# Retention and a gated feed-forward block on one core: another order of the last output products, and of two weight loads at the start

## The chip, the core and the metric

The program runs on one core of a Trainium2 chip. The core has five engines with queues of their own that run at the same time and wait for each other by semaphores. TensorE (PE in the profile; PEld is its loading of weights) multiplies matrices and writes only to PSUM, an accumulating memory of eight banks. VectorE (DVE) does elementwise work, ScalarE (ACT) copies and functions such as softplus and erf, GpSimd (POOL) elementwise work too. SyncE (SP) issues DMA transfers, ScalarE's queue can issue some as well. "SPq" and "ACTq" stand for these queues. Data lie in SBUF, 128 partitions wide; inputs and outputs in DRAM.

The metric is the device time of one execution in microseconds.

## The reference

```python
# attention: 8 batches, 8 heads, 576 tokens, head dim 64
scores = scale * np.matmul(q, k.transpose(0, 1, 3, 2))
gamma = 1.0 - 2.0 ** (-5.0 - np.arange(H))
Dmat = np.where(rel >= 0, gamma ** rel, 0.0)       # rel = position of q - position of k
x = matmul(scores * Dmat, v)                       # -> (4608 tokens, 512)
# feed-forward
h = x @ w_in                                       # 512 -> 2048
sp = np.maximum(h, 0.0) + np.log1p(np.exp(-np.abs(h)))
g = h * erf(sp)
out = g @ w_out                                    # 2048 -> 512
```

q, k and v are float32. w_in and w_out come as 64-bit floats, and the kernel gets them as raw words: it makes float32 of them itself, which the code calls rounding.

## The kernel before, in words

**Attention.** The 4608 tokens are 36 pieces of 128 (each ninth piece is two rests of 64 tokens). A piece goes through three stages: `transposes` (q and k of the piece are turned on TensorE, line 332, or from piece 8 on in part on VectorE, line 326), `scores` (line 347, then VectorE's masking into `sT`, line 99 through the helper `tt`), and `outputs` (lines 365, 376, 388, with a state that is carried from piece to piece). `outputs` writes the piece's columns of `x`, four pieces to a chunk of 512 tokens, nine chunks. The list `stages` fixes the order: transposes of piece i+1, outputs of i, scores of i+1 (outputs first for pieces 5 and 7). `transposes(i)` asks for q of piece i+2, `outputs(i)` for k and v of piece i+3. Each is two DMAs on SyncE's queue (line 147), of 128 KB each; q has two buffers in turn, k and v four. From piece 8 on q, and from piece 12 on k, come in other pieces (line 131).

**Feed-forward.** w_in's 2048 columns are worked in four groups `g` of 512; for each group all nine chunks are passed. `First` is the stage x @ w_in with what follows it up to g, `Second` the product with w_out, added to an output tile `o` that goes through DRAM (`od`) from group to group. Most of these products are done as seven products of half-size blocks, with sums of blocks before and after (names such as A11, S1, B21, T2). `First.plain`, used for the first two chunks of group 0, is the ordinary product instead: sixteen steps, four for each 128 rows of w_in (`dc` 0 to 3). It can so begin with the first part of w_in while the others still come.

**Weights.** `parts()` lists the pieces of weights: for each group four parts of w_in (128 rows, two DMAs of 256 KB, line 237) and four of w_out (one DMA of 512 KB). `load_weights` asks for the next part, into one of four buffers `wraw`. `round_weights(5)` makes one part into float32 with ScalarE (lines 254, 255) and VectorE (lines 259, 263, 267, 272), and for w_in of group 0 two more operations on VectorE (lines 274, 275), else on GpSimd.

**Order at the start.** Everything up to the end of the first chunk's plain product is in an order written out by hand, a string read character by character: "a" is the next stage of attention, "p" a step of the plain product, "w" `load_weights`, a digit so many steps of `round_weights`, "k" two idle matmuls that keep TensorE busy, "l" a load of k and v, "c" the second half of the constants, "s" a store of x. Nothing reorders instructions after that; each engine and each queue takes its own in program order.

**The end.** Line 806 runs the last second stage: chunk 8 of group 3. `first` gives the products B11 and B21, `rest` then T2, T3, T1, T4 and B22. Each product is four calls of 128x256 matmuls on TensorE (line 604; eight records in the profile), into a PSUM bank that holds two blocks of 128 tokens (`tp` 0 and 1), each 256 columns wide. B11, T2, T1 and B22 accumulate in bank `a`, B21 in bank `e`, T3 and T4 in bank `g`. After each product one VectorE addition of 128x512 (`take` or `add`, line 99) adds the bank to `o`. `store` writes results to the output in DRAM (line 688 for this chunk): columns 0 to 255 of half 0 on ScalarE's queue after T3, half 1 on SyncE's after T4, the rest of half 0 on both queues after B22.

Of the kernel before, what the change touches and what calls it, by code (L numbers as in the profile page):

```python
# [11 lines left out]
FP32 = mybir.dt.float32  # L12
# [3 lines left out]
ALU = mybir.AluOpType  # L16
PSUM = bass.MemoryType.PSUM

P = 128
B, H, S, D = 8, 8, 576, 64  # L20
D_MODEL, D_FF = 512, 2048
NP = H // 2
# [32 lines left out]
def kernel(  # L55
# [10 lines left out]
    nc = tc.nc  # L66
# [3 lines left out]
    TH = TCH // 2  # L70
    n_ch = n_tok // TCH
    n_dc = D_MODEL // P
    OH = D_MODEL // 2
    FH = D_FF // 2
    GP = 2
# [14 lines left out]
    ps_at = ctx.enter_context(tc.tile_pool(name="ps_at", bufs=4, space=PSUM))  # L90
# [7 lines left out]
    def tt(out, in0, in1, op):  # L98
        nc.vector.tensor_tensor(out=out, in0=in0, in1=in1, op=op)  # L99

    def flat(ap):
        return ap.rearrange("p h d -> p (h d)")
# [47 lines left out]
    def load(i, names="qkv"):  # L150
        if i < len(pieces):
            t = loaded.setdefault(i, {})
            for name in names:
                src = {"q": q, "k": k, "v": v}[name]
                if name == "q" and i < SQUARES:
                    t["q"] = load_rows(i, "q", q, 2)
                elif name == "q":
                    t["qs"] = load_squares(i, "q", q)
                    if i >= SQUARES_K:
                        t["ks"] = load_squares(i, "k", k)  # L160
                elif name == "v" or i < SQUARES_K or len(pieces[i]) == 1:
                    t[name] = load_rows(i, name, src, 4)
# [19 lines left out]
    B11, T3, B21, B22, T1, T2, T4 = range(7)  # L182
    weights = {}
# [48 lines left out]
    def load_weights():  # L232
        part = next(coming, None)
        if part is not None:
            t = wraw.tile([P, 2 * WP], UINT32, tag="wraw", name="wraw")
            for rows, src in part[0]:
                nc.sync.dma_start(out=t[rows].rearrange("p (h f) -> p h f", h=2), in_=src)
            words.append((t, *part[1:]))
# [49 lines left out]
    def round_weights(n=1):  # L288
        for _ in range(n):
            next(round_step, None)  # L290
# [151 lines left out]
    def before_chunk(c):  # L442

        return stages.index((outputs, c * PC)) if c < n_ch else len(stages)

    def after_chunk(c):

        return stages.index((outputs, (c + 1) * PC - 1)) + 1

    def attend(upto):  # L450
        while done[0] < min(upto, len(stages)):
            of, i = stages[done[0]]
            of(i)
            done[0] += 1
# [5 lines left out]
    def load_x(g, c):  # L460
        x[g, c] = x_tile()
        nc.sync.dma_start(out=x[g, c][:, :n_dc], in_=xd[c])

    def store_x(c):
        nc.sync.dma_start(out=xd[c], in_=x[0, c][:, :n_dc])
# [3 lines left out]
    def operands_x(g, c):  # L469
        summed.add((g, c))  # L470
        t = x[g, c]
        b11, b12, b21, b22 = (t[:, 2 * d : 2 * d + 2, h * TH : (h + 1) * TH] for d in range(2) for h in range(2))
        t1, t2, t4 = (t[:, n_dc + j, :].rearrange("p (d i) -> p d i", d=2) for j in range(3))
        if g == 0 or c < PLAIN:
            tt(t1, b12, b11, ALU.subtract)
            tt(t2, b22, t1, ALU.subtract)
            tt(b12, b22, b12, ALU.subtract)
        else:
            tt(t2, b12, b11, ALU.add)
            tt(t1, b22, t2, ALU.subtract)  # L480
        if g == 0:
            store_x(c)
        tt(t4, b21, t2, ALU.subtract)
        x[g, c] = {A11: b11, A12: b21, S4: b22, A22: t4, S1: t1, S2: t2, S3: b12}
# [102 lines left out]
    class Second:  # L587
# [58 lines left out]
        def last(self):  # L646
# [6 lines left out]
            self.store(1)  # L653
            yield

        def rest(self):


            e = ps_e.tile([P, 2, OH], FP32, tag="g", name="g2")
            self.product(T2, self.a, False)  # L660
            self.take(1, 0, self.a)
            yield
            self.product(T3, e, True)
            self.add(1, 1, e)
            self.store(0, slice(0, OH), nc.scalar)
            yield
            self.product(T1, self.a, False)
            self.take(1, 1, self.a)
            yield
            self.product(T4, e, False)  # L670
            self.add(1, 0, e)
            self.store(1)
            yield
            self.product(B22, self.a, False)
            self.take(0, 1, self.a)
            for tp, queue in enumerate((nc.sync, nc.scalar)):
                self.store(0, slice(OH, D_MODEL), queue, (tp,))
            yield
# [29 lines left out]
    def keep_busy(n):  # L708
        for _ in range(n):
            nc.tensor.matmul(idle[:, :P], lhsT=ones, rhs=ones, start=True, stop=True)  # L710
# [4 lines left out]
    def run(steps, rounds=(), stages=1):  # L715

        for step, _ in enumerate(steps):
            attend(min(done[0] + stages, most[0]))
            round_weights(rounds[step] if step < len(rounds) else 0)
# [4 lines left out]

    for what in "alkakakawkakakawaa3awwa2aaa5ppappawwppa5ppaw5appwcppa5ppaaapp5s":
        if what == "a":
            attend(done[0] + 1)
        elif what == "p":  # L730
            next(products)
        elif what == "s":
            store_x(0)
        elif what == "l":
            load(2, "kv")
        elif what == "c":
            nc.sync.dma_start(out=cst[:, CONST_FIRST:], in_=consts[:, CONST_FIRST:])
        elif what == "w":
            load_weights()
        elif what == "k":  # L740
            keep_busy(2)
        else:
            round_weights(int(what))
# [18 lines left out]
    for b, nxt in zip(blocks[2:], blocks[3:] + [None]):  # L762
        n = order.index((b.g, b.c))
        if isinstance(b, First):
            most_g[0] = order[n - 1][0] + 1
            run(b.middle(), (1, 1) if n != 2 else ())
            firsts[n - 1].sums()
            run(seconds[n - 1].first(), (1, 1) if n > 2 else ())
            run(b.last(), (1,) if 2 < n < n_ch else ())
            if n in (2, 3):  # L770
                load_weights()
            most[0] = before_chunk(n + 3)
        elif n + 2 < n_s:
            f = firsts[n + 1]
            for step, _ in enumerate(b.middle()):
                attend(min(done[0] + 1, most[0]))
                if step == 0:
                    f.erf()
                elif step == 1 and (n + 2 >= n_ch or done[0] == len(stages)):
                    operands_x(*order[n + 2])  # L780
                elif step == 2 and n_ch - 4 < n < n_ch:
                    round_weights()
            if order[n + 2] not in summed:
                attend(after_chunk(n + 2))
                operands_x(*order[n + 2])
            run(nxt.first(), (1,) if n > 1 else ())
            f.multiply()
            seconds[n + 1].begin()
            if n_ch <= n + 3 < n_s:
                load_x(*order[n + 3])  # L790
            run(b.last(), (0, 1) if n > 1 else ())
        elif n + 1 < n_s:
            firsts[n + 1].erf()
            seconds[n + 1].begin()
            rest = b.rest()
            for _ in range(3):
                next(rest)
            firsts[n + 1].multiply()
            run(rest)
            firsts[n + 1].sums((0,))  # L800
            first = nxt.first()
            next(first)
            firsts[n + 1].sums((1,))
            run(first)
        else:
            run(b.rest())


# [28 lines left out]
```

## Time and profile before

| | us |
|---|---|
| median of eight runs (1026.51 to 1031.78) | 1027.68 |
| profiled execution, own time | 1031.78 |
| profiled execution, span | 1030.0 |
| TensorE busy | 1019.2 |
| VectorE busy | 668.9 |
| ScalarE busy | 390.3 |
| GpSimd busy | 124.1 |
| one product of a second stage, chain on TensorE | 1.73 |
| addition of 128x512 on VectorE, in the groups `o<-a,o` | 0.69 |

The page has busy times by engine, and a strip of 40 equal slices of the span (25.75 us each):

```profile
PE   9989999999999999999999999999999999999998
PEld 8778888888888888888888888888888888888887
DVE  3858877877876666666566666666667655555555
ACT  2254133232244544343343344444443333333332
POOL 2133121221311110000001001100100000000000
PEclk9999999999999999999999999999999999999999
DMA  9998979979984444444445344444333334444433
```

A digit is the busy share of the slice in tenths. PEclk is the clock that TensorE was granted, in tenths. DMA is the share of the sixteen DMA engines. Attention's stages lie between the products in the first slices up to about 270 us; after that only feed-forward is left. A TensorE that is shown as busy can still be slower than it could be, since ends of matmuls are modelled.

### The profile page before, as it was taken

To read this page: it belongs to the slowest core of one execution; us is meant where nothing else is said; L and a number is where in the kernel's file an instruction comes from. 1 tells how busy PE (TensorE), PEld (TensorE's weight loads), DVE (VectorE), ACT (ScalarE), POOL (GpSimd) and SP (SyncE) were. 2 spreads that over 40 slices of the span, in tenths; PEclk is the share of its full clock that TensorE was granted. 3 is DMA by queue.
4 is the path that set the end of the run, shared out by engine and by line. 5 is a ranking of instruction groups with operands and counts; after the bars stand their busy time and mean duration, and the time that the engine had idled before them with its cause. 6 is when DMAs were issued, how large, how long until landed. Compare 5 with 4: busy or idle time off the path is not lost.

```text
span 1030.0 us, 15950 instructions
## 1 busy us (share of the span) xinstructions
PE 1019.2 (99%) x6348; PEld 876.7 (85%) x6348; DVE 668.9 (65%) x1055; ACT 390.3 (38%) x481; POOL 124.1 (12%) x122
## 2 busy tenths in 40 slices
PE   9989999999999999999999999999999999999998
PEld 8778888888888888888888888888888888888887
DVE  3858877877876666666566666666667655555555
ACT  2254133232244544343343344444443333333332
POOL 2133121221311110000001001100100000000000
PEclk9999999999999999999999999999999999999999
DMA  9998979979984444444445344444333334444433
GB/s 194 182 238 184 231 165 241 236 170 247 221 192 150 163 143 143 143 163 163 162 144 172 137 143 147 159 165 143 143 123 123 123 127 131 130 131 133 125 95 110
DMA packets 146986, 165.76 MB, mean 161 GB/s; under 512 B 97376, under 2 KB 121568, under 8 KB 138848
## 3 DMA queue, kind: packets, MB, share of 16 engines
q1 hardware_dynamic: 144848, 163.70, 55.9%
q10 hardware_dynamic: 2064, 1.05, 0.4%
q8 instruction: 50, 0.82, 0.3%
q14 instruction: 24, 0.20, 0.1%
HBM read 117.52 MB, written 47.19 MB: 160 GB/s over the span
## 4 chain that ended last, share of the span: by engine, by line
PE 87%; DMA 6%; SPq 3%; DVE 2%; issue 1%; ACT 0%; POOL 0%; DVEq 0%; ACTq 0%; POOLq 0%
PE a L604 23%; PE a L496 22%; PE g L604 11%; PE g L496 11%; PE e L604 6%; PE e L496 5%; PE s L347 2%; PE o L365 2%; SPq L147 2%; DMA raw_k<-in_k_dram 1%; DMA raw_ks<-in_k_dram 1%; DMA raw_qs<-in_q_dram 1%; DMA wraw<-in_moe_w_in_dram 1%; PE o L388 1%; PE p L550 1%; PE o L376 1%
## 5 line engine op out<-in xcount | busy, mean ns | idle before, releaser
L496 PE MATMUL a<-x,wa 128*128 128x256 f32 x1088 | 258.3, 380 | 0.0
L496 PEld LDWEIGHTS a<-x,wa 128*128 128x128 f32 x1088 | 205.7, 190 | 28.5
L604 PE MATMUL a<-wb,s 128*128 128x256 f32 x864 | 205.7, 381 | 0.0
L604 PEld LDWEIGHTS a<-wb,s 128*128 128x128 f32 x864 | 162.9, 190 | 23.6 <-ACT o L618 0.7
L99 DVE TENSOR_TENSOR t<-g,t 128x512 f32<-128x512 f32 x68 | 47.0, 691 | 150.5 <-ACT t L526 113.0
L496 PE MATMUL g<-x,wa 128*128 128x256 f32 x544 | 129.2, 380 | 0.0
L496 PEld LDWEIGHTS g<-x,wa 128*128 128x128 f32 x544 | 102.8, 190 | 14.4
L99 DVE TENSOR_TENSOR o<-a,o 128x512 f32<-128x512 f32 x108 | 74.3, 688 | 49.2 <-PE a L604 49.2
L521 ACT COPY t<-a 128x512 f32<-128x512 f32 x34 | 19.9, 586 | 188.3 <-PE a L496 188.3
L99 DVE TENSOR_TENSOR t<-t,s 128x1024 f32<-128x1024 f32 x72 | 88.9, 1276 | 0.0
L565 ACT ACTIVATE s<-t 128x1024 f32<-128x1024 f32 x72 | 72.1, 1049 | 27.8 <-DVE t L99 27.8
L274 POOL TENSOR_TENSOR wraw<-wraw 128x512 f32<-128x512 f32 x28 | 29.4, 1050 | 438.5 <-DVE wraw L272 179.1
L99 DVE TENSOR_TENSOR x<-x 128x512 f32<-128x512 f32 x115 | 75.8, 693 | 1.2
L532 ACT COPY t<-a 128x512 f32<-128x512 f32 x34 | 19.9, 586 | 144.4 <-PE a L496 144.4
L569 ACT ACTIVATE s<-s 128x1024 f32<-128x1024 f32 x72 | 72.1, 1048 | 0.4
L604 PE MATMUL g<-wb,s 128*128 128x256 f32 x288 | 68.6, 381 | 0.0
L604 PE MATMUL e<-wb,t 128*128 128x256 f32 x288 | 68.5, 380 | 0.0
L604 PE MATMUL a<-wb,t 128*128 128x256 f32 x288 | 68.5, 380 | 0.0
L604 PE MATMUL g<-wb,t 128*128 128x256 f32 x288 | 68.2, 380 | 0.0
L99 DVE TENSOR_TENSOR sT<-s,cst 128x512 f32<-128x512 f32 x72 | 46.2, 682 | 30.7 <-PE s L347 28.5
L99 DVE TENSOR_TENSOR o<-g,o 128x512 f32<-128x512 f32 x72 | 49.4, 686 | 24.6 <-ACT o L618 19.8
L496 PE MATMUL e<-x,wa 128*128 128x256 f32 x272 | 64.8, 381 | 0.0
(76 smaller groups left out, 1229.1 us busy)
## 6 DMA issues: line engine op xcount, KB each, us to landing
od<-o SPq DMA_DIRECT2D x54, 512.0 KB, 3.3
x<-xd SPq DMA_DIRECT2D x27, 1024.0 KB, 4.8
o<-od SPq DMA_DIRECT2D x27, 1024.0 KB, 4.9
raw_qs<-in_q_dram SPq DMA_DIRECT2D x96, 112.0 KB, 4.5
raw_ks<-in_k_dram SPq DMA_DIRECT2D x84, 112.0 KB, 4.2
xd<-x SPq DMA_DIRECT2D x9, 1024.0 KB, 4.9
raw_v<-in_v_dram SPq DMA_DIRECT2D x64, 128.0 KB, 4.6
wraw<-in_moe_w_in_dram SPq DMA_DIRECT2D x32, 256.0 KB, 5.9
```

The costliest lines, as they stand in the source:

```text
L99: nc.vector.tensor_tensor(out=out, in0=in0, in1=in1, op=op)
L147: queue.dma_start(out=t[r0 : r0 + n, e::2, :], in_=heads.rearrange("h p d -> p h d"))
L274: engine.tensor_tensor(out=r_f, in0=high_f, in1=r_f, op=ALU.mult)
L347: nc.tensor.matmul(ps[e][:, p, :], lhsT=t["kT"][heads[e], p, :], rhs=t["qT"][heads[e], p, :], start=True, stop=True)
L365: nc.tensor.matmul(o[p % 2][heads[(e + p) % 2], p // 2, :], lhsT=t["v"][:, 2 * p + e, :], rhs=t["sT"][:, e, p, :], start=(p < 2), stop=(no ...
L376: nc.tensor.matmul(o[p % 2][heads[(e + p) % 2], p // 2, r0 : r0 + m], lhsT=state[heads[e], p, :], rhs=t["qT"][heads[e], p, r0 : r0 + m], s ...
L496: nc.tensor.matmul(acc[:, j * TH : (j + 1) * TH], lhsT=weights["wa", self.g][:, a, d, j * P : (j + 1) * P], rhs=x[self.g, self.c][a][:, d, :],
L521: nc.scalar.copy(out=self.t1[:, 1], in_=self.a)
L532: nc.scalar.copy(out=self.t2[:, 0], in_=self.a)
L565: nc.scalar.activation(self.s[:, j], t, AF.Softplus)
L569: nc.scalar.activation(self.s[:, j], self.s[:, j], AF.Erf)
L604: nc.tensor.matmul(acc[:, tp, :], lhsT=left[:, j * TH + tp * P : j * TH + (tp + 1) * P], rhs=weights["wb", self.g][:, b, j, :], start=(sta ...
```

## The change

Two things are changed. At the start, three characters of the string move. "w" for the third part of w_in comes directly after that for the second, ahead of the loads of q, k and v of piece 5; the fourth keeps its place. The rounding of the third part ("5") comes before the scores of piece 5 instead of after them, and that of the fourth after those scores, before the outputs of piece 5, instead of after the outputs. TensorE's own order at the start stays as it was.

At the end, `final` replaces `first` and `rest` for the last second stage. The products keep their order, but the two blocks of 128 tokens have banks of their own: two banks for B11, T2, T1 and B22 and two for B21, T3 and T4, all from the pool `ps_at` that attention has used before. For each product block 0 is done whole, then block 1; each has its own addition of 128x256. The stores are by block as well: block 0 on SyncE's queue, block 1 on ScalarE's, after B21 (half 0, columns 0 to 255), T4 (half 1) and B22 (half 0, the other columns).

```diff
+        def final(self):
+            a = [ps_at.tile([P, NP, P], FP32, tag="at", name=f"f{tp}") for tp in range(2)]
+            e = [ps_at.tile([P, NP, P], FP32, tag="at", name=f"h{tp}") for tp in range(2)]
+            steps = [(B11, a, 0, 0), (B21, e, 0, 0), (T2, a, 1, 0), (T3, e, 1, 1)]
+            steps += [(T1, a, 1, 1), (T4, e, 1, 0), (B22, a, 0, 1)]
+            for n, (b, banks, half, oh) in enumerate(steps):
+                left = self.of.left[b]
+                for tp in range(2):
+                    acc = flat(banks[tp])[:, :OH]
+                    for j in range(GP):
+                        nc.tensor.matmul(
+                            acc,
+                            lhsT=left[:, j * TH + tp * P : j * TH + (tp + 1) * P],
+                            rhs=weights["wb", self.g][:, b, j, :],
+                            start=(b in (B11, B21, T3) and j == 0),
+                            stop=(j == GP - 1),
+                            skip_group_check=True,
+                        )
+                    dst = self.o[:, half, tp, oh * OH : (oh + 1) * OH]
+                    tt(dst, acc, dst, ALU.add)
+                    if b in (B21, T4, B22):
+                        cols = slice(0, D_MODEL) if half == 1 else slice(oh * OH, (oh + 1) * OH)
+                        self.store(half, cols, (nc.sync, nc.scalar)[tp], (tp,))
+                yield n
...
-    for what in "alkakakawkakakawaa3awwa2aaa5ppappawwppa5ppaw5appwcppa5ppaaapp5s":
+    for what in "alkakakawkakakawwaa3awa2aaa5ppappa5wwppa5ppawappwcppa5ppaaapp5s":
...
-            first = nxt.first()
-            next(first)
+            steps = nxt.final()
+            next(steps)
             firsts[n + 1].sums((1,))
-            run(first)
+            next(steps)
         else:
-            run(b.rest())
+            run(steps)
```

## The prediction

> **What bounds the kernel now.** I read the busy shares first, then who waits for whom on TensorE, then the timeline of the first 75 us and of the last 7 us, because the change touches only these two ends. All times are of the profiled execution: span 1030.0 us, its own time 1031.78 us (1.78 us around the span). The median of the eight runs, 1027.68 us, lies 4.1 us lower, so the profiled execution has more waiting in it than the usual one. I work out differences in it and set them against the median.
>
> The page's first part, and the waits of TensorE (us in total, times, longest):
>
> ```profile
> PE 1019.2 (99%) x6348; PEld 876.7 (85%) x6348; DVE 668.9 (65%) x1055; ACT 390.3 (38%) x481; POOL 124.1 (12%) x122
> ```
>
> ```profile
> PE pt_k L332 <- DMA raw_k<-in_k_dram: 3.0, 3, 2.2
> ...
> PE s L347 <- ACT kT L338: 1.0, 2, 0.7
> ...
> PE p L550 <- DVE wa L275: 0.3, 1, 0.3
> ```
>
> TensorE is busy for 1019.2 of 1030.0 us. The missing 10.8 us are some 4.1 us after the last matmul, 0.6 us between 200 and 300 us, and the rest in the first 75 us. No window between 75 and 200 us or from 300 to 1000 us has idle time. So only the beginning and the tail can move the time.
>
> The beginning, timeline (start us, us, engine, line, what):
>
> ```profile
> 22.72 1.19 SPq L237 DMA_DIRECT2D wraw<-in_moe_w_in_dram  x2
> 24.01 1.90 SPq L147 DMA_DIRECT2D raw_q<-in_q_dram  x2
> 25.95 1.27 SPq L147 DMA_DIRECT2D raw_k<-in_k_dram  x2
> 27.32 4.53 SPq L147 DMA_DIRECT2D raw_v<-in_v_dram  x2
> ...
> 31.89 2.48 SPq L237 DMA_DIRECT2D wraw<-in_moe_w_in_dram  x4
> ...
> 32.91 0.63 PE L332 MATMUL pt_k<-ident,raw_k 128*128 128x128 f32 x4 [0.43 <-DMA raw_k<-in_k_dram]
> ```
>
> The second part of w_in is asked for at 22.72 us, then q, k and v of piece 5, then the third and fourth part together. The transposes of piece 5 on TensorE (pt_q 31.82, pt_k 32.91 us) come as soon as their q and k have landed (31.7 and 32.8 us): this place is already bound by the load, with no reserve.
>
> The chain of work between 38 and 52 us (start, us, what):
>
> ```profile
> 39.82 1.27 DVE sT L99 x2
> 41.09 0.35 DVE wa L259
> ...
> 49.51 0.70 DVE wa L275
> 50.22 0.04 issue
> 50.26 1.78 PE p L550 x7
> ```
>
> Here VectorE is the chain: masked scores of piece 5, rounding of the third part, three small operations, rounding of the fourth, and only then the plain product that needs the fourth part. But TensorE has other work meanwhile; it loses only 0.34 us at 50.26.
>
> The last load wait, chain, and three windows around it (us; PE busy (x), PEld, DVE, ACT, POOL, granted clock, DMA share, GB/s):
>
> ```profile
> 64.68 5.20 DMA raw_k<-in_k_dram
> 69.88 0.14 issue
> 70.02 0.63 PE pt_k L332 x4
> ```
>
> ```profile
> 67.40:70.80 3.40, 1.17 (x8) 0.79 (x7) 0.21 (x1) 3.39 (x4) 0.12 (x1) 1.00 1.26 315
> 70.80:74.20 3.40, 3.40 (x13) 2.31 (x13) 3.22 (x5) 2.29 (x5) 1.25 (x1) 0.50 1.14 285
> 74.20:77.60 3.40, 3.40 (x56) 2.67 (x54) 2.44 (x5) 0.00 (x0) 0.65 (x1) 1.00 0.99 354
> ```
>
> TensorE stands still for 2.23 us until k of piece 9 has landed, and then gets half the clock for 3.4 us, which costs up to another 1.7 us. This is the largest single loss of the beginning.
>
> The tail:
>
> ```profile
> 1023.96 1.89 PE L604 MATMUL a<-wb,s 128*128 128x256 f32 x8
> ...
> 1024.88 1.57 SPq L688 DMA_DIRECT2D out_dram<-o  x3
> 1025.89 0.69 DVE L99 TENSOR_TENSOR o<-a,o 128x512 f32<-128x512 f32 x1 [1.03 <-PE a L604]
> ```
>
> The last add follows the last matmul by 0.04 us, then come the two last stores: issued at 1026.6, landed 2.4 us (SyncE) and 2.1 us (ScalarE) later, so at 1029.0 and 1028.7. The span ends 1.0 us after that.
>
> **The change, part by part.**
>
> *1. Last second stage, TensorE.* The same 28 matmuls in the same order of products, 8 records of 1.73 us a product. New is that the two of one token block follow each other into one region. Line 496 does just that, at 380 ns, against 381 ns for line 604: cost 0.
>
> *2. Its adds on VectorE.* Seven of 128x512 (0.69 us) become fourteen of 128x256 (0.42 us, the next one 0.33 us later, by x<-o of 128x256): 0.75 for 0.69 us a product, hidden under 1.73 us of TensorE. Where a bank is used again, one product lies between. The tightest is the fourth product, which now opens the banks that the second one filled. VectorE begins the first add at 1015.75: 0.75 for it, 1.29 for the two sums behind it, 0.75 for the second add, done at 1018.5; the product begins at 1018.95. Reserve 0.45 us; if it is gone, up to +0.3, so bounds 0 to +0.3. I take 0. The four banks belong to the attention's pool, free for hundreds of us.
>
> *3. The end.* The last block's add is 0.42 instead of 0.69 us, done at 1026.31. Its store is ScalarE's and lands 2.1 us after issue: 1028.44. The other block's matmuls end half a product (0.86 us) earlier; its store on SyncE, issued at 1025.45, lands by 1027.9. The stores of the product before leave sooner and on two queues, so SyncE isn't blocked by them (in before its last issue took 0.48 us behind three others). Last landing 1028.44 instead of 1029.0: -0.6 us. Bounds: 0 (if landings there are set by the data in flight), -0.8 (if the landing shrinks to 2.0 us, the shortest there, and the wait behind it too).
>
> *4. The loads on SyncE.* The third part's two DMAs pass the six DMAs of q, k, v of piece 5; SyncE's list is the same again from the fourth part on. All four buffers for raw weights are free, so the moved ones wait for no buffer. What they cost piece 5: least, their issue, 1.3 us (row 31.89: 2.48 for four). Most, what a second pair adds when it stands directly behind another: of the four issued from 31.89 on, the second landed 7.3 us after 32.48 (39.8) and the fourth 8.9 us after 33.77 (42.7): 2.9 us. I take 2.9, since that row is the same pair of transfers in the same place of a pair. The DMA share of 0.84 between 30 and 35 us speaks for a little less.
>
> *5. What waits for it.* q of piece 5 lands at 34.6, k at 35.7. TensorE stands before pt_q from 31.8 to 34.6 and again before pt_k: +2.9 us. In order behind it: two plain products, outputs of piece 4, the next products, scores of piece 5.
>
> *6. The roundings on VectorE.* The third part's six operations (0.43, 0.44, 0.70, 0.45, 0.70, 0.69 us: 3.4) now stands before the masked scores of piece 5, the fourth's before the three operations of its outputs. After the delay of 2.9 us VectorE is through with piece 4 at about 40.4, rounds until 43.8, and the masked scores (1.3 us) end at 45.1; TensorE has finished the two products behind the scores at 44.5: a new wait of 0.6 us. ScalarE's two operations for a part (1.3 us) wait for landings (33.9 and 42.0, estimates from the same rows), with only copies needed after 46 us behind them. Delay 3.5 us.
>
> *7. What the delay swallows.* Loads and roundings are now ahead of TensorE: the waits at 44.74 (0.2), 50.26 (0.3), 56.05 (for kT, 0.7) and 59.17 (weight load for raw_v, 0.4) go, as ScalarE and GpSimd are tied there to the w_out parts, which come when they came before. Left 1.9 us. TensorE then reaches the transpose of piece 9 at 67.8 + 1.9 = 69.7, and k of piece 9 lands at 69.88 as before, since SyncE from 47 to 64.7 us is paced by landings of the same list. So the new wait at 32 us takes the place of the old one at 70 us: sum 0 at 70 us, as long as the delay is under 2.2 us there.
>
> *8. The half clock.* In the profiled execution the 1.7 us after 70.8 us may go, as its wait shrinks to 0.2 us. Or it comes at 35 us instead, because the new wait of 2.8 us is longer than the 2.23 that led to it: +1.7 there, 0.2 of it hidden, against -1.7. Bounds for the beginning: -1.7 to +1.5 (the latter where the usual run has no half clock at 70 us). The middle of these is -0.1; I take 0.
>
> The Trainium skill, "TensorE: Matmul & The Clock Gate", section "HAM oscillation — how this bites in real kernels", gives gaps of over some 3.4 us as what brings the half clock. By it neither 2.23 nor 2.8 us would, and step 8 would be 0. The trace has it after 2.23 us of standing still in a window of 3.4 us (granted clock 1.00, then 0.50), so the measurement decides, and the rule's silence about the new wait isn't to be trusted.
>
> Sum: 0 - 0.6 = -0.6 us: 1031.2 for the profiled execution, 1027.1 for the median.
>
> **The rivals.**
>
> *A, faster.* The old wait and its half clock go and no half clock comes at 32 us: -1.7 - 0.6 = -2.3: 1025.4. For it: the wait at 70 us nearly vanishes by step 7. It would reach 1024.4 if k of piece 9 also came 1 us sooner. Against: the usual run is 4.1 us faster than the profiled one, so it may have no half clock to lose.
>
> *B, slower.* One mechanism: the wait at 32 us is not paid back at 70 us, because in usual runs k of piece 9 is already there in time. It decides once the wait at 70 us is under 1.9 us: with none at all, +1.9 - 0.6 = +1.3: 1029.0; with the half clock after the new wait, +3.0: 1030.7. The gap of 4.1 us speaks for it, the DMA share of 1.26 before 70 us against.
>
> *C, it doesn't do what it says.* The third part fills idle DMA time, piece 5 is late by 1.3 us only, which vanishes at 70 us; and the tail's landing is set by the data: 1027.7.
>
> **How the numbers follow.** Chances: forecast 50%, A 20%, B 20%, C 10%. The forecast's own range is 1026.3 to 1028.0 (tail 0 to -0.8, k of piece 9 half a us either way). The range takes in most of A and the lower part of B: 1025.2 to 1029.5. About 0.2%, 2.06 us, is what a measurement here can tell: faster means below 1025.6, slower above 1029.7. Below: somewhat over three fifths of A and a little of the forecast, 17%; above: three fifths of B, 12%; I give 18 and 13.
>
> **What would show it.** Right: after's timeline has a wait before pt_q of some 2 to 3 us near 32 us, led by a DMA of q or k; no wait for wa L275; the wait at raw_k near 70 us under 1 us; the last adds 128x256 of 0.42 us and the last landing some 2.1 us after them. Wrong: no new wait at 32 us (step 4), a wait of the product behind h banks (step 2), a first steady product, now at 88.2 us, that comes over 1 us earlier or later (steps 7 and 8).

## The result, and the profile after

The changed kernel takes 1030.23 us (median of 13 executions, 1028.05 to 1032.06), the kernel before 1027.36 us (36 executions, 1026.34 to 1031.78): a ratio of 1.0026, 95% interval 1.0019 to 1.0033. It is slower by 2.7 us by the ratio and 2.9 us by the medians, where 0.6 us less was forecast.

The two profiled executions do not show that. Both have a span of 1030.0 us; their own times are 1031.74 us (after) and 1031.78 us (before). So the first thing to explain is why two profiles that agree stand for medians that differ.

The waits of TensorE in the changed kernel (us in total, times, longest):

```profile
PE pt_q L332 <- DMA raw_q<-in_q_dram: 2.7, 1, 2.7
...
PE s L347 <- DVE kT L326: 0.9, 1, 0.9
PE s L347 <- DVE qT L326: 0.3, 1, 0.3
PE s L347 <- ACT kT L338: 0.2, 1, 0.2
```

The wait for k of piece 9 (2.2 us) and the one for wa L275 are gone, and a wait of 2.7 us for q has come. Its place, in the timeline of SyncE's queue and of TensorE:

```profile
22.52 3.42 SPq L237 DMA_DIRECT2D wraw<-in_moe_w_in_dram  x4
26.04 1.09 SPq L147 DMA_DIRECT2D raw_q<-in_q_dram  x2
27.54 1.59 SPq L147 DMA_DIRECT2D raw_k<-in_k_dram  x2
```

```profile
29.56 1.99 PE L550 MATMUL p<-x,wa 128*128 128x256 f32 x8
34.23 1.09 PE L332 MATMUL pt_q<-ident,raw_q 128*128 128x128 f32 x4 [2.68 <-DMA raw_q<-in_q_dram]
35.43 1.09 PE L332 MATMUL pt_k<-ident,raw_k 128*128 128x128 f32 x4
36.30 1.67 PE L550 MATMUL pe<-x,wa 128*128 128x256 f32 x4
```

Four DMAs of w_in stand together now, q of piece 5 is asked for 2 us later, and TensorE stands still from 31.5 to 34.2 us. The four transposes then take 1.09 us instead of 0.63 and the plain product 1.67 instead of 1.03. The windows say why (us; PE busy (x), PEld, DVE, ACT, POOL, granted clock, DMA share, GB/s):

```profile
30.80:34.20 3.40, 0.75 (x4) 0.33 (x3) 2.33 (x6) 1.23 (x2) 0.00 (x0) 1.00 0.68 124
34.20:37.60 3.40, 3.26 (x12) 2.65 (x13) 1.19 (x2) 1.58 (x3) 0.76 (x1) 0.50 0.78 178
37.60:41.00 3.40, 3.40 (x41) 2.85 (x40) 1.05 (x3) 1.30 (x3) 0.28 (x1) 1.00 1.21 176
```

The half clock that before's profile had from 70.8 to 74.2 us now lies from 34.2 to 37.6 us. The wait and its place are as steps 4 and 5 of the prediction had them, the half clock as the second of the two cases of step 8.

The end, timeline:

```profile
1024.40 1.89 PE L668 MATMUL f<-wb,s 128*128 128x256 f32 x8
...
1025.46 0.43 DVE L99 TENSOR_TENSOR o<-f,o 128x256 f32<-128x256 f32 x1 [0.44 <-PE f L668]
1026.33 0.42 DVE L99 TENSOR_TENSOR o<-f,o 128x256 f32<-128x256 f32 x1 [0.44 <-PE f L668]
```

The last addition is 0.42 instead of 0.69 us. From the last matmul's end (1026.3) to the end of the span 3.7 us pass; in before it was 4.1 us.

### The profile page after: what moved, and what is told of

The parts are those of the page before. It is cut to its first block, busy times and chain, and to the rows that moved or that the text cites. A ratio compares the mean times of both kernels' runs of the same rounds, so it can differ in the third digit from the quotient of the medians.

```text
span 1030.0 us, 15959 instructions
## 1 busy us (share of the span) xinstructions
PE 1020.2 (99%) x6348; PEld 877.8 (85%) x6348; DVE 668.7 (65%) x1062; ACT 390.1 (38%) x481; POOL 123.4 (12%) x122
## 4 chain that ended last, share of the span: by engine, by line
PE 87%; DMA 5%; DVE 3%; SPq 2%; ACT 1%; issue 1%; POOL 1%; ACTq 0%; DVEq 0%; POOLq 0%
PE a L604 23%; PE a L496 22%; PE g L496 11%; PE g L604 11%; PE e L604 6%; PE e L496 5%; PE o L365 2%; PE s L347 2%; DMA wraw<-in_moe_w_in_dram 1%; DMA raw_ks<-in_k_dram 1%; PE o L388 1%; PE o L376 1%; DMA raw_v<-in_v_dram 1%; SPq L147 1%; PE f L668 1%
## 5 line engine op out<-in xcount | busy, mean ns | idle before, releaser
L604 PE MATMUL a<-wb,s 128*128 128x256 f32 x840 | 200.0, 381 | 0.0
L604 PEld LDWEIGHTS a<-wb,s 128*128 128x128 f32 x840 | 158.4, 190 | 22.9 <-ACT o L618 0.7
L99 DVE TENSOR_TENSOR o<-a,o 128x512 f32<-128x512 f32 x104 | 71.6, 688 | 46.4 <-PE a L604 46.4
```

Of the source, the lines that this page charges most:

```text
L604: nc.tensor.matmul(acc[:, tp, :], lhsT=left[:, j * TH + tp * P : j * TH + (tp + 1) * P], rhs=weights["wb", self.g][:, b, j, :], start=(sta ...
```

## The experiments

The theory after the result: the start loses the time. The moved load makes TensorE wait for q of piece 5, the half clock follows in most executions, and in a usual execution of the kernel before there is no wait near 70 us that could pay this back. The rivals: the ending costs it; the roundings ahead of attention's operations on VectorE cost it; the wait is paid back and something else is the loss.

**The kernel before again**

No edit.

> The kernel before, unchanged, for a second profiled execution. The profiled execution of before took 1031.78 us, 4.4 us more than the median of 1027.4. Theory (the new wait is not paid back): in a usual execution k of piece 9 is there nearly in time, so the wait of TensorE near 70 us is under 1 us and no half clock follows; time 1027.4 us. Rival (paid back): the wait near 70 us is again about 2.2 us, and the half clock is again there.

Measured: median 1027.91 us against 1027.72 for the same kernel beside it (ratio 1.0005, 0.9995 to 1.0015). The profiled execution took 1029.94 us, again over the median. It has the wait, but a shorter one, and no half clock behind it:

```profile
65.59 1.03 PE L550 MATMUL p<-x,wa 128*128 128x256 f32 x4
68.08 0.63 PE L332 MATMUL pt_k<-ident,raw_k 128*128 128x128 f32 x4 [1.47 <-DMA raw_k<-in_k_dram]
```

Neither expectation is met: 1.47 us lies between them, and the execution is not a usual one by its time. Its mean clock is 0.999, so a mean clock near 1 does not by itself say that the wait is missing. The run shows only that this wait changes from one execution to another. It was left to the other runs to say what a usual execution has.

**The ending alone, and the start alone**

The ending alone is the changed kernel with the old string:

```diff
-    for what in "alkakakawkakakawwaa3awa2aaa5ppappa5wwppa5ppawappwcppa5ppaaapp5s":
+    for what in "alkakakawkakakawaa3awwa2aaa5ppappawwppa5ppaw5appwcppa5ppaaapp5s":
```

The start alone is the kernel before with the new string:

```diff
-    for what in "alkakakawkakakawaa3awwa2aaa5ppappawwppa5ppaw5appwcppa5ppaaapp5s":
+    for what in "alkakakawkakakawwaa3awa2aaa5ppappa5wwppa5ppawappwcppa5ppaaapp5s":
```

> Only the new ending (four banks, additions of 128x256, stores by block); the start as before. Theory (the loss comes from the start, the ending gains its 0.6 us): 1026.8 us. Rival (the ending costs the time, through its additions, its banks or its stores): 1030 us or more.

> Only the new order at the start (load and roundings); the ending as before. Theory (the start costs it): 1030.8 us, the changed kernel's median and 0.6 us. Rival (the ending costs it): at most 1027.9 us.

Measured: the ending alone 1026.88 us (0.9992, 0.9981 to 1.0003), the start alone 1030.36 us (1.0030, 1.0018 to 1.0042), beside 1027.72 us. The whole loss is the start's; the ending costs nothing.

**Only the load is moved**

```diff
-    for what in "alkakakawkakakawaa3awwa2aaa5ppappawwppa5ppaw5appwcppa5ppaaapp5s":
+    for what in "alkakakawkakakawwaa3awa2aaa5ppappawwppa5ppaw5appwcppa5ppaaapp5s":
```

> Of the start only the load of the third part is moved ahead of piece 5's q, k and v; both roundings keep their old places; the ending as before. Theory (the load delays q and k of piece 5): a wait of about 2.7 us before pt_q near 34 us, and 1030.2 to 1030.8 us. Rival (the roundings ahead of the masked scores cost it): the wait may be there, but is paid back, and the time is at most 1028.2 us.

Measured: 1030.47 us (1.0029, 1.0019 to 1.0039), as much as the whole start. TensorE's timeline in its profile:

```profile
33.36 0.63 PE L332 MATMUL pt_q<-ident,raw_q 128*128 128x128 f32 x4 [2.08 <-DMA raw_q<-in_q_dram]
34.54 0.63 PE L332 MATMUL pt_k<-ident,raw_k 128*128 128x128 f32 x4 [0.55 <-DMA raw_k<-in_k_dram]
```

The wait for q and k is 2.6 us together. This execution has full clock throughout and still takes 1030.05 us. So the load alone brings the loss, and the half clock is not the whole of it: only two of these seven executions have a mean clock of 0.998 or less, and the other five have a median of 1030.05 us. Of the six executions of the start alone five have 0.998 or less, so equal medians do not yet say that the moved roundings cost nothing; what they do is read from the profiles below.

**TensorE kept busy in the new wait**

```diff
-    for what in "alkakakawkakakawwaa3awa2aaa5ppappa5wwppa5ppawappwcppa5ppaaapp5s":
+    for what in "alkakakawkakakawwaa3awa2aaa5ppbappa5wwppa5ppawappwcppa5ppaaapp5s":
...
+        elif what == "b":
+            spare = [ps_at.tile([P, NP, P], FP32, tag="at", name=f"spare{n}") for n in range(2)]
+            for n in range(12):
+                nc.tensor.matmul(spare[n % 2][:, 0, :], lhsT=ones, rhs=ones, start=True, stop=True)
```

> The changed kernel, with twelve matmuls of ones (128x128, some 2.6 us on TensorE) into two spare banks just ahead of piece 5's transposes, so that TensorE works through the new wait instead of standing still. Nothing reads their result. Theory (new wait, and the half clock that it brings in most executions): no half clock near 35 us, 1028.5 us, 1.7 less than the changed kernel's 1030.2. Rival (the half clock does not matter, all of the loss is the wait): 1030.2 us or more.

Measured: 1029.44 us (1.0018, 1.0010 to 1.0027), beside 1027.27 us. The matmuls of ones fill the wait, and the transposes have full clock again:

```profile
31.63 2.84 PE L772 MATMUL spare<-ones 128*128 128x128 f32 x24
34.31 0.60 PE L332 MATMUL pt_q<-ident,raw_q 128*128 128x128 f32 x4
34.74 0.60 PE L332 MATMUL pt_k<-ident,raw_k 128*128 128x128 f32 x4
```

The mean granted clock is known for every execution. One half-clock window of 3.4 us in 1028 us makes it 0.998. Of the changed kernel's 13 executions ten have 0.998 or less, with a median of 1030.6 us; the other three took 1028.05, 1028.85 and 1029.24 us. With the matmuls of ones all eleven have 0.999 or 1.000. So the half clock is really tied to standing still. The median is 0.8 us lower, less than the 1.7 us expected, and the intervals of the two ratios overlap, so the times alone do not show the gain. A reason that fits, but that no run tests, is that the matmuls themselves hold TensorE for 2.8 us in every execution, also where the wait would have been shorter.

**The price doubled**

```diff
-    for what in "alkakakawkakakawwaa3awa2aaa5ppappa5wwppa5ppawappwcppa5ppaaapp5s":
+    for what in "alkakakawkakakawwwaa3aa2aaa5ppappa5wwppa5ppawappwcppa5ppaaapp5s":
```

> The changed kernel with the price doubled: the fourth part of w_in too is asked for ahead of q, k and v of piece 5, so that second, third and fourth part stand together. Theory (each part ahead of piece 5 delays its q and k by 2 to 3 us, and nothing later pays it back): a wait near 34 us of about 5 us in all, and 1032.2 to 1033.2 us. Rival (the loss has another cause than the place of the load): as the changed kernel, 1030.2 us.

Measured: 1033.17 us (1.0057, 1.0044 to 1.0069), 2.9 us over the changed kernel. The wait in its profile:

```profile
36.18 1.09 PE L332 MATMUL pt_q<-ident,raw_q 128*128 128x128 f32 x4 [4.49 <-DMA raw_q<-in_q_dram]
```

Two parts moved ahead of piece 5 lose about twice what one loses (5.9 against 2.9 us over the kernel before), and two half-clock windows in a row can follow (0.996 in two of five executions).

**The payback by itself**

The kernel before with the same twelve matmuls of ones ahead of piece 5's transposes:

```diff
-    for what in "alkakakawkakakawaa3awwa2aaa5ppappawwppa5ppaw5appwcppa5ppaaapp5s":
+    for what in "alkakakawkakakawaa3awwa2aaa5ppbappawwppa5ppaw5appwcppa5ppaaapp5s":
```

> The kernel before with the same twelve matmuls of ones (some 2.6 us of work) ahead of piece 5's transposes: TensorE is made late there without any load being moved, without standing still and without a half clock. It measures the payback alone. Theory (in a usual execution there is no wait near 70 us to pay back with; only some 1 us of small waits at 45 to 60 us swallows a part): 1029.0 to 1029.4 us. Rival (the wait near 70 us pays it back): at most 1027.9 us.

Measured: 1029.28 us (1.0019, 1.0010 to 1.0028), beside 1027.27 us. The matmuls hold TensorE for 2.8 us, with no load moved and no half clock, and cost 2.0 us of median. The profile, with that of the ending alone from its second run (below, 1027.00 us) beside it, shows where the difference goes. With the matmuls of ones:

```profile
30.09 1.99 PE L550 MATMUL p<-x,wa 128*128 128x256 f32 x8
...
35.03 0.60 PE L332 MATMUL pt_k<-ident,raw_k 128*128 128x128 f32 x4
...
68.88 0.60 PE L332 MATMUL pt_k<-ident,raw_k 128*128 128x128 f32 x4
```

Without them:

```profile
29.40 2.00 PE L550 MATMUL p<-x,wa 128*128 128x256 f32 x8
...
32.15 0.63 PE L332 MATMUL pt_k<-ident,raw_k 128*128 128x128 f32 x4 [0.32 <-DMA raw_k<-in_k_dram]
...
66.03 0.60 PE L332 MATMUL pt_k<-ident,raw_k 128*128 128x128 f32 x4
```

The execution with the matmuls is 0.69 us late already before them (30.09 against 29.40). At pt_k of piece 5 it is 2.88 us late, so the matmuls themselves add 2.2 us; most of the rest falls into the wait for k, which is gone. At the transpose of piece 9 it is 2.85 us late: from pt_k on nothing is paid back.

**The wait near 70 us taken away**

The ending alone, and the last part of w_out asked for after k and v of piece 9:

```diff
-    for what in "alkakakawkakakawaa3awwa2aaa5ppappawwppa5ppaw5appwcppa5ppaaapp5s":
+    for what in "alkakakawkakakawaa3awwa2aaa5ppappawwppa5ppaw5appcppa5ppaaawpp5s":
```

> The new ending with the old start, but the last part of w_out of group 0 is asked for after k and v of piece 9 instead of before them, so that k of piece 9 lands some 2 us sooner and the wait near 70 us goes. Theory (usual executions have no such wait): the wait is gone from the profiled execution, but the median stays at that of the new ending alone, 1026.5 to 1026.9 us. Rival (the wait is there in usual executions): 1025.0 to 1025.5 us.

Measured: 1026.91 us (0.9993, 0.9984 to 1.0002). The transpose of piece 9 starts without a wait, and the median stays at that of the ending alone. Its profiled execution took 1026.91 us, just its median.

**The ending once more, beside the version that keeps what helped**

The version above, with the fourth part's rounding ahead of the outputs of piece 5:

```diff
-    for what in "alkakakawkakakawaa3awwa2aaa5ppappawwppa5ppaw5appcppa5ppaaawpp5s":
+    for what in "alkakakawkakakawaa3awwa2aaa5ppappawwppa5pp5awappcppa5ppaaawpp5s":
```

> The version with the new ending and the late last part of w_out, and in addition the one piece of the change at the start that moves no load: the fourth part of w_in is rounded before the outputs of piece 5. The third part's load and rounding stay where the kernel before has them. Theory (all that the start loses comes from the load): the wait of 0.8 us for wa L275 near 50 us goes, and the time is 1026.1 to 1026.6 us, below both kernels. Rival (rounding ahead of attention's operations on VectorE costs as much as it gains): 1026.9 us or more.

> The new ending alone once more, beside the version above, to narrow its interval. Theory (the ending gains 0.5 us, as the time from the last matmul to the end of the span shows, 3.63 against 4.15 us): 0.4 to 0.8 us under the kernel before. Rival (no gain in usual executions): within 0.2 us of it.

Measured, beside 1027.40 us: this version 1026.04 us (0.9985, 0.9976 to 0.9994), under both kernels. Its profile has no wait for wa L275; the product that needs the fourth part starts right behind the scores:

```profile
47.83 1.16 PE L347 MATMUL s<-qT,kT 64*128 64x128 f32 x16
48.92 1.99 PE L550 MATMUL p<-x,wa 128*128 128x256 f32 x8
```

The ending alone again: 1026.75 us (0.9997, 0.9988 to 1.0006). Its medians lie 0.84 and 0.65 us under the kernel before's, but both intervals hold 1, so the gain is clear only in the profiles: from the last matmul's end to the end of the span 3.5 to 3.7 us in all seven profiles with the new ending, 4.1 to 4.2 us in all five with the old one.

This second run of the ending gave the missing view. It is one kernel in two profiled executions. The first, 1030.76 us, TensorE's timeline:

```profile
65.45 1.03 PE L550 MATMUL p<-x,wa 128*128 128x256 f32 x4
69.13 0.63 PE L332 MATMUL pt_k<-ident,raw_k 128*128 128x128 f32 x4 [2.66 <-DMA raw_k<-in_k_dram]
69.59 1.85 PE L550 MATMUL p<-x,wa 128*128 128x256 f32 x4
```

The second, 1027.00 us:

```profile
65.16 1.03 PE L550 MATMUL p<-x,wa 128*128 128x256 f32 x4
66.03 0.60 PE L332 MATMUL pt_k<-ident,raw_k 128*128 128x128 f32 x4
66.46 1.03 PE L550 MATMUL p<-x,wa 128*128 128x256 f32 x4
```

TensorE comes to this place at about the same time (65.2 and 65.5 us). In the first execution k of piece 9 isn't there for another 2.7 us, and the half clock follows (products of 1.85 instead of 1.03 us). In the second it has landed. The second is within 0.3 us of the median (1026.75 us), the first 3.9 us above its own (1026.88 us), so the second is taken for the usual one.

## Why the prediction was wrong

**The step that failed is 7**, "what the delay swallows". It let the wait of 2.23 us near 70 us pay for the new one, because the profile of before had that wait. The profiled execution was not a usual one: at 1031.78 us it is the slowest of the 36. Of the kernel before's 74 timed executions beside the experiments, three have a mean clock of 0.998 (1030.19, 1031.34, 1031.81 us); the others have 0.999 or 1.000 and a median of 1027.4 us. In a usual one of those there is no wait near 70 us to pay with, as the second profile of the ending alone shows; the medians of the payback run and of the late last part say the same. For each execution by itself it is not shown. Rival B named this mechanism with its price, 1029.0 us, and 1030.7 us with the half clock; the median lies between. It had 20%, although the gap of 4.1 us between profile and median was noted and even given as what speaks for it.

The same step let small waits between 44 and 60 us swallow 1.6 us more. Against the ending alone at 1027.00 us, the kernel before with the matmuls of ones starts pt_k of piece 5 2.88 us later, the transpose of piece 9 2.85 us later and the first product with w_out 2.86 us later (85.80 against 82.94). Nothing of the delay is swallowed on that way. Those waits too were in part the slow load stream's: the waits for kT are 1.0 us in all in the profile of before and 0.3 us in the one at 1027.00 us. Only the wait for wa L275 went, through the moved rounding. Nor did k of piece 9 land "as before": in the changed kernel's profile it is there at 65.3 us, against 69.9 us in the profile of before, and TensorE gets to it only at 70.2 us.

**Step 8**, the half clock, was right in kind and wrongly priced at 0. By the mean clocks it comes in ten of the thirteen executions, and they take 1.7 us more than the other three (1030.6 against 1028.85 us). The row that step 8 had weighed above the Trainium skill, "TensorE: Matmul & The Clock Gate", section "HAM oscillation — how this bites in real kernels", holds: 2.66 and 2.68 us of standing still brought the half clock here, well under the page's 3.4 us; 1.47 us did not. The length of a single wait does not settle it, though: in the profile of the start alone the half clock came behind two waits of 0.99 and 1.98 us with one transpose between them, and in that of the load alone it did not come behind 2.08 and 0.55 us.

**The other steps** held, or were off by 0.5 us at most. Step 1: a product is 1.73 us as before. Step 2: the second product's additions end at 1018.8, the fourth product starts at 1019.2 us, no wait. Step 3: the ending gains 0.5 us (4.15 to 3.63 us) instead of 0.6. Step 4: the wait for q is 2.7 us against 2.8; but as the old wait for k goes, the load by itself delays TensorE by 2.4 us and not by 2.9 (the first product with w_out starts at 85.33 us in the profile of the load alone, which has full clock, against 82.94 us). Step 5: q lets TensorE go at 34.2 us, 34.6 was forecast. Step 6: the third part's rounding ahead of the masked scores costs TensorE 0.7 us; 0.6 was forecast. The way from the last product ahead of the outputs of piece 5 (pg) to the transpose of piece 6, in the profile of before:

```profile
40.67 1.03 PE L550 MATMUL pg<-x,wa 128*128 128x256 f32 x4
41.62 1.09 PE L365 MATMUL o<-sT,raw_v 128*64 128x128 f32 x16
...
43.86 0.66 PE L332 MATMUL pt_q<-ident,raw_q 128*128 128x128 f32 x4
```

and in the changed kernel, where the masked scores `sT` come later:

```profile
44.24 1.03 PE L550 MATMUL pg<-x,wa 128*128 128x256 f32 x4
44.55 1.28 DVE L99 TENSOR_TENSOR sT<-s,cst 128x512 f32<-128x512 f32 x2
45.34 1.64 PE L365 MATMUL o<-sT,raw_v 128*64 128x128 f32 x16
...
48.12 0.66 PE L332 MATMUL pt_q<-ident,raw_q 128*128 128x128 f32 x4
```

It takes 3.88 instead of 3.19 us, most of it inside L365, so that the table of waits does not show it. All four profiles with that rounding moved have 3.88 us, the eight others 3.19 or 3.20. So the two moved roundings together come out about even: +0.7 and -0.8 us.

The sum, done again by what the runs show: 2.4 us by which the load delays TensorE and that nothing pays back, 1.7 us of half clock in ten of thirteen executions (1.3 on average), +0.7 for the masked scores, -0.8 for the wait for wa L275, -0.5 for the ending: +3.1 us. Measured: 1030.23 - 1027.36 = +2.9 us, with an interval of 2.0 to 3.4 us by the ratio. Several terms come from single profiles, so the agreement is better than they are known.

What stays open is why the load stream is some 4 us slower in some executions of one and the same kernel. The three profiles that show it (the kernel before twice, the ending alone once) are all of executions above their medians; no run tells whether the profiling or something else brings it on. The chip may have a part in it: two of the three were taken on one chip, where three of 26 executions of the kernel before have a mean clock of 0.998; on two other chips none of 48 has, and the second profile of the ending alone is from one of these. Where the first profile of before was taken is not on record. The rest of the program varies as well: from the first product with w_out to the start of the last product the twelve profiles take 935.6 to 937.5 us, the kernel before alone 935.8 and 937.5 us. So the span of a single profile cannot show a difference of 1 us.

## What to carry to other kernels

Before a wait in the profile is used to pay for a new one, see whether the profiled execution is a usual one: here it was 4 us over the median, and what made it so was the wait that was counted on. A load that is moved forward in a queue is paid by the first consumer behind it that is already just in time, and standing still for 2.7 us on TensorE cost another 1.7 us through the clock in most executions. Moving the work that consumes a load took away a wait of 0.8 us for the fourth part's rounding, and cost 0.7 us for the third part's, for which the masked scores had to wait; moving the load lost more than the work could gain.

## What was not expected of the hardware

One and the same kernel had k of piece 9 ready before 66.0 us in one execution and only at 69.0 us in another, with the same instructions in the queue. TensorE's granted clock fell to 0.50 for 3.4 us behind 2.66 us of standing still and stayed at 1.00 behind 1.47 us; behind 4.49 us it was 0.50 for some 6.8 us (35.6 to 42.4 us). But it was so for as long (34.7 to 41.5 us) in the profile of the start alone, behind 0.99 and 1.98 us with a transpose of 0.63 us between, and stayed at 1.00 behind 2.08 and 0.55 us in that of the load alone. What decides between them is not shown.
